# Two heads side by side in a clustered attention kernel: one run of probabilities times v for both

## The chip, the cores and the metric

The kernel runs on one core of one Trainium2 chip. The time is the device time of one execution in microseconds (us); three executions were timed. The core has five engines with queues of their own: TensorE (PE; its weight loads are listed apart as PEld), VectorE (DVE), ScalarE (ACT), GpSimd (POOL) and SyncE (SP), which issues the DMAs here. TensorE writes its results to PSUM, and VectorE and ScalarE carry them from there to SBUF.

## What is computed

```
def _attn_ref(q, k, v, centroids):            # q, k, v: (2, 8, 768, 64)
    ...
    q_assign = np.argmax(np.einsum('bhsd,hcd->bhsc', q_n, c_n), axis=-1)
    k_assign = np.argmax(np.einsum('bhsd,hcd->bhsc', k_n, c_n), axis=-1)
    mask = q_assign[:, :, :, None] == k_assign[:, :, None, :]
    scores = scale * np.matmul(q, k.transpose(0, 1, 3, 2))
    scores = np.where(mask, scores, -1000000000.0)
    ...                                        # softmax over the keys
    return np.matmul(attn, v)
# then x (1536, 512): softmax-gated layer with normalisation (w_in, w_out),
# then (x @ w_a) * (x @ w_b) @ w_out2
```

Every query and key is put to one of 16 clusters of its head; a query sees the keys of its own cluster only. Two feed-forward layers follow.

## The kernel before

Batch 2 and 8 heads make eight pairs of heads `(b, hp)`. A sequence of 768 is six tiles of 128. A step `i` is one query tile `t` of one head `j` of one pair `n`, called a head-tile below; there are 96, and the list `steps` sets their order: before, all six tiles of head 0, then all six of head 1, then the next pair.

A step has these parts. `score`: four matmuls (L992) into one of two PSUM buffers `psS`, with the cluster mask as further rows of the operands; then VectorE takes the negated row maximum (L996) and ScalarE the exponential with its row sum (L1000) into one of two buffers of probabilities. `turn`: six transposes (L1024), three into the PSUM bank `psT0` and three into `psT1` (printed as psT_67 and psT_68, and the score buffers as psS_65 and psS_66); of each step the first half is copied out by VectorE (L1031) and the second by ScalarE (L1033), into a buffer of transposed probabilities at `PT_`. `apply`, for a group of three tiles (384 queries) of one head: part 1 (L1048) multiplies v by the transposed probabilities, six matmuls of 128x384 with 64 output columns, one for each key tile `kt`. They alternate between the two halves of the array's columns, so that even key tiles are summed in PSUM rows 0 to 63 of `psO` and odd ones in rows 64 to 127. Each of these f32 matmuls is two instructions in the profile. Part 2 adds the two half sums: ScalarE copies one (L1061) and VectorE adds the other (L1062). Part 3, once per group of a pair, divides by the row sums (transposes L1077, product L1080) and splits the result into two fp32r parts for the next layer.

Before each pair its queries and keys are prepared (`prep`): loads (L658), transposes (L729 into `psM`; for the very first pair L763), split into a high and a low part (ACT L736, POOL L737 and L739, or DVE L746), similarities to the centroids (L819, L823; for the first pair L788, reduced by L791), the arg-max as one-hot rows (L857 to L874), their transposes (L902, for the first pair L883), and DMAs that place the parts in the operand slots of each head (`do_place`, L805; one-hot rows `do_ohd`, L912). There are four such slots, two pairs of heads.

No order of instructions is written out. Every operation is added to a list with its engine, a cost, a rank, and what it reads and writes (`pl.add`). A list scheduler runs through the list with these costs and takes, on each engine, the operation of lowest rank among those whose inputs are there; what it finds is the program order of each engine. The rank is that of the task (in steps: `SUB`, `LEAD`, `OFF`) plus entries of the table `ADJ`. At run time each engine goes through its list in order and waits at semaphores.

The layers behind attention (`moe_h`, `moe_ln`, `moe_x2`, `moe2_ab`, `moe2_y`; L1139, L1212, L1229, L1282, L1310) keep TensorE busy to the end; weights are split by ScalarE, VectorE and GpSimd before.

## Time and profile before

| | |
|---|---|
| median of three executions | 719.59 us (719.44 to 1163.23) |
| the profiled execution | 717.53 us, span 715.5 us |
| TensorE busy | 697.1 us, 97% of the span |
| VectorE, ScalarE, GpSimd busy | 437.1, 345.4, 264.6 us |
| granted TensorE clock | 0.996 |
| attention ends (last apply run) | about 286 us |

One of the three executions took 1163.23 us; the other two agree within 0.2 us. Busy times are of the profiled execution. A matmul's duration there is the time until its result is there; since matmuls are pipelined, what it costs is read from the distance between the starts of two.

### The profile page before, as it was taken

What the parts mean: (1) busy time and instruction counts of PE and PEld (TensorE: products, weight loads), DVE (VectorE), ACT (ScalarE), POOL (GpSimd) and SP (SyncE); (2) the same over time, 40 slices, a digit from 0 to 9 for tenths busy, and PEclk for the clock granted to TensorE, in tenths of its full rate; (3) what the DMA queues carried; (4) which work ended last, traced back from release to release, by engine and by line L of the source; (5) the groups of instructions that cost most, each with busy time, mean ns of one, the idle gap of its engine ahead of it and who ended that gap; (6) DMA issues with size and microseconds to landing.
All of it is one profiled execution on the core that took longest, in us unless ns stands there. A gap on an engine that the chain in (4) does not pass through costs nothing.

```text
span 715.5 us, 10716 instructions
## 1 busy us (share of the span) xinstructions
PE 697.1 (97%) x3960; PEld 569.0 (80%) x3960; DVE 437.1 (61%) x752; ACT 345.4 (48%) x679; POOL 264.6 (37%) x295
## 2 busy tenths in 40 slices
PE   7898999999999999899999999999999999999997
PEld 6766776787777767788999998888888888888886
DVE  5877777888779868898997269851344211111212
ACT  5766676787777764665356234442242211121111
POOL 2246441456464314557364078950354300000000
PEclk9999999999999999999999999999999999999999
DMA  4647437174716201313223032340020000010011
GB/s 156 155 104 192 133 93 184 49 177 125 204 29 168 70 31 66 112 60 117 89 60 120 1 119 83 124 147 1 22 67 30 1 0 1 0 60 1 20 40 59
DMA packets 39091, 58.46 MB, mean 82 GB/s; under 512 B 3832, under 2 KB 33920, under 8 KB 39040
## 3 DMA queue, kind: packets, MB, share of 16 engines
q1 hardware_dynamic: 39040, 57.79, 28.1%
q8 instruction: 31, 0.51, 0.3%
q14 instruction: 20, 0.16, 0.1%
HBM read 36.74 MB, written 3.15 MB: 56 GB/s over the span
## 4 chain that ended last, share of the span: by engine, by line
PE 83%; DVE 6%; ACT 5%; DMA 2%; issue 1%; SPq 1%; POOL 1%; DVEq 0%; ACTq 0%; POOLq 0%
PE psT L1282 14%; PE psS L1310 14%; PE psS L992 7%; PE psT L1024 7%; PE psO L1282 7%; PE psM L1282 7%; PE psO L1048 7%; PE psS L1139 5%; PE psM L1229 5%; PE psO L1229 5%; ACT F L1000 2%; PE psM L819 1%; PE psT L1212 1%; PE psM L729 1%; DVE mxn L996 1%
## 5 line engine op out<-in xcount | busy, mean ns | idle before, releaser
L472 POOL TENSOR_TENSOR R<-F,R 128x512 fp32r<-128x512 f32 (+1 forms) x68 | 88.0, 1302 | 97.9 <-ACT R L598 77.0
L1282 PE MATMUL psT<-R 128*128 128x512 f32 x432 | 103.5, 389 | 0.0
L1310 PE MATMUL psS<-R 128*128 128x512 f32 x432 | 103.3, 389 | 0.0
L1000 ACT ACTIVATE F<-psS,mxn 128x768 f32<-128x768 f32 x96 | 86.8, 905 | 20.1 <-DVE mxn L996 17.0
L996 DVE TENSOR_REDUCE mxn<-psS 128x1 f32<-128x768 f32 x96 | 90.7, 950 | 7.9 <-PE psS L992 5.3
L1310 PEld LDWEIGHTS psS<-R 128*128 128x128 f32 x432 | 81.1, 188 | 16.8
L1282 PEld LDWEIGHTS psT<-R 128*128 128x128 f32 x432 | 81.0, 188 | 16.7
L992 PE MATMUL psS<-R 128*128 128x512 f32 (+3 forms) x384 | 91.9, 362 | 0.7 <-ACT F L1000 0.7
L1024 PE MATMUL psT<-ident,F 128*128 128x128 f32 x576 | 86.1, 276 | 1.8 <-ACT F L1000 1.4
L589 POOL TENSOR_TENSOR F<-F 128x512 int32<-128x512 int32 x45 | 63.8, 1422 | 34.3 <-DVE F L585 19.6
L1024 PEld LDWEIGHTS psT<-ident,F 128*128 128x128 f32 x576 | 65.4, 141 | 12.8 <-ACT F L1000 7.8
L992 PEld LDWEIGHTS psS<-R 128*128 128x128 f32 (+1 forms) x384 | 65.9, 192 | 11.1 <-ACT F L1000 1.8
L1295 ACT CAST R<-F 128x512 fp32r<-128x512 f32 x36 | 22.5, 624 | 104.1 <-PE psS L1310 102.2
L1296 DVE TENSOR_TENSOR R<-F,R 128x512 fp32r<-128x512 f32 x36 | 32.9, 914 | 64.4 <-ACT R L1295 64.3
L1139 PE MATMUL psS<-R 128*128 128x512 f32 x288 | 68.7, 393 | 2.0 <-DVE F L1160 2.0
L1048 PE MATMUL psO<-F 128*64 128x384 f32 x384 | 69.0, 494 | 0.0
L1139 PEld LDWEIGHTS psS<-R 128*128 128x128 f32 x288 | 53.1, 188 | 13.4 <-DVE F L1160 2.2
L1031 DVE COPY F<-psT 128x384 f32<-128x384 f32 x96 | 52.7, 549 | 12.3 <-PE psT L1024 11.9
L1033 ACT COPY F<-psT 128x384 f32<-128x384 f32 x96 | 45.9, 478 | 27.2 <-PE psT L1024 22.8
L1293 ACT COPY F<-psT 128x512 f32<-128x512 f32 x36 | 21.1, 586 | 66.7 <-PE psT L1282 64.2
L579 POOL TENSOR_SCALAR F<-F 128x512 int32<-128x512 uint32 x45 | 32.5, 722 | 54.5 <-DMA F<-in_moe_w_b_dram 12.3
L1282 PE MATMUL psO<-R 128*128 128x512 f32 x216 | 51.9, 389 | 0.0
(148 smaller groups left out, 1021.4 us busy)
## 6 DMA issues: line engine op xcount, KB each, us to landing
F<-in_moe_w_out_dram SPq DMA_DIRECT2D x20, 512.0 KB, 3.2
R<-R SPq DMA_DIRECT2D x28, 288.0 KB, 4.2
F<-in_moe_w_b_dram SPq DMA_DIRECT2D x12, 512.0 KB, 3.5
F<-in_moe_w_a_dram SPq DMA_DIRECT2D x12, 512.0 KB, 4.0
R<-R SPq DMA_DIRECT2D x28, 192.0 KB, 4.6
F<-in_moe_w_in_dram SPq DMA_DIRECT2D x8, 512.0 KB, 5.1
F<-in_v_dram SPq DMA_DIRECT2D x8, 384.0 KB, 4.5
out_dram<-F SPq DMA_DIRECT2D x12, 256.0 KB, 2.1
```

Source lines behind the costliest of these rows:

```text
L472: pl.add("POOL", pool(n), rank, lambda: G.tensor_tensor(out=out_, in0=in0, in1=in1, op=ALU.subtract), reads, writes)
L589: pl.add("POOL", pool(n), rank, lambda: G.tensor_tensor(out=u, in0=u, in1=low, op=ALU.add), [rk, lwk], [uk])
L992: T.matmul(sp[:, c0:c0 + cn], kq[:r, 2 * m, t * P:(t + 1) * P], kq[:r, 2 * m + 1, c0:c0 + cn], start=m == 0, stop=m == 1)
L996: pl.add("DVE", dve(S), i + SUB["max"], lambda: V.tensor_reduce(out=mxn[:, b:b + 1], in_=sp[:, :S], axis=AX.X, op=ALU.max, negate=True), [ ...
L1000: pl.add("ACT", act(S) + 93 + 93, i + SUB["exp"], lambda: A.activation(F[:, po:po + 768], sp[:, :S], AF.Exp, bias=mxn[:, b:b + 1], scale=1 ...
L1024: T.transpose(sp[:, c, :], pt[:, kt * P:(kt + 1) * P], ident)
L1031: pl.add("DVE", dve(HN), rk, lambda sp=sp, dh=dh: V.tensor_copy(dh, sp), [sk], [hk])
L1048: T.matmul(psO[rs, :AN], vs[:, j, kt % HT * 2 + kt // HT], pt[:, kt, :], start=kt < 2, stop=kt >= NT - 2, tile_position=(0, kt % 2 * D), s ...
L1139: T.matmul(sp[:, n0:n0 + 512], xv5[:, i, a, c], winv[:, w, c, n0:n0 + 512], start=first, stop=(c == KD - 1 and a == 1))
L1229: T.matmul(sp[:, :GN], wo1v(f, w)[:, ds_], d[a][:, f, :], start=(f == 0 and x == 0), stop=(f == NF1 - 1 and x == 2))
L1282: T.matmul(pt, w[:, l, c, :], xv5[:, xs, a, c, :], start=first, stop=(c == KD - 1 and l == 1))
L1310: T.matmul(yv[t][0], hl2[a][:, ts_], wo[:, l, :], start=(first and a == 0 and l == 0), stop=(last and a == 1))
```

## The change

The steps run in another order: three tiles of head 0, the same three of head 1, then the other three of each. The transposed probabilities of the group lie in two buffers, one for each head, where before two buffers were used in turn for consecutive groups. One apply run follows for the group of both heads: twelve matmuls, of which those of head 0 use the first half of the array's columns and those of head 1 the second. Each half of `psO` then holds the whole sum of one head, and part 2 is one ScalarE copy of 128x384. The run's rank puts it directly behind the last turn, where it had been two steps later. Head 1's placing DMAs get an earlier rank. All entries of `ADJ` are other numbers; two stand here for all.

```
-LEAD = {... 'p1': -5.424, ...}
+LEAD = {... 'p1': -8.0, ...}
...
-    "apply1 0 PE": -123.885, "apply1 1 PE": 0.157, "apply1 2 PE": 9.015, "apply1 3 PE": 421.761,
...
-PVC = 6 * 324.0 + 260.0
+PVC = 12 * 324.0 + 260.0
...
-                rk = r0 + LEAD["p1" if j else "p0"] + part * 0.01
+                rk = max(r0 + LEAD["p1" if j else "p0"], 12 * n - 14.0) + part * 0.01
...
-    steps = [(n, j, t) for n in range(NPR) for j in range(2) for t in range(NT)]
+    steps = [(n, j, g * GA + t) for n in range(NPR) for g in range(NG) for j in range(2) for t in range(GA)]
...
-    def pto(n, j, g):
-        return PT_ + (n * 4 + j * 2 + g) % 2 * 2304
+    def pto(j):
+        return PT_ + j * 2304
...
-                for kt in range(NT):
-                    rs = slice(kt % 2 * D, (kt % 2 + 1) * D)
-                    T.matmul(psO[rs, :AN], vs[:, j, kt % HT * 2 + kt // HT], pt[:, kt, :], start=kt < 2, stop=kt >= NT - 2,
-                             tile_position=(0, kt % 2 * D), skip_group_check=True)
-
-            pl.add("PE", PVC, i + SUB["pv"] + 2, mm, [fc((o, NT * AN), (VS[n % 2] + j * 384, 384))], ["psO"], after=70.0)
+                    for j in range(2):
+                        T.matmul(psO[j * D:(j + 1) * D, :AN], vs[:, j, kt % HT * 2 + kt // HT],
+                                 F[:, pto(j) + kt * AN:pto(j) + (kt + 1) * AN], start=kt == 0, stop=kt == NT - 1,
+                                 tile_position=(0, j * D), skip_group_check=True)
+
+            pl.add("PE", PVC, i + SUB["t1"] + 0.1, mm, [fc((PT_, 2 * NT * AN), (VS[n % 2], 768))], ["psO"], after=70.0)
...
-            pl.add("ACT", act(AN) + 110, rk, lambda: A.copy(xv[hi], psO[lo, :AN]), ["psO"], [hk])
-            pl.add("DVE", dve(AN), rk, lambda: V.tensor_tensor(
-                out=xv[hi], in0=psO[hi, :AN], in1=xv[hi], op=ALU.add), ["psO"], [hk])
+            pl.add("ACT", act(AN), i + 3 + SUB["mg"], lambda: A.copy(xv, psO[:, :AN]), ["psO"], [xk])
...
-        if t % GA == GA - 1:
-            task(i + SUB["pv"] + 2, apply, i, 1)
+        if j and t % GA == GA - 1:
+            task(i + SUB["t1"] + 0.1, apply, i, 1)
```

What that does to the order of instructions is shown at three places. The first is TensorE before head 1 of the first pair is scored. Of before, from the similarity transposes of the second pair (L823) to the first apply run; the last score run there (L992) is head 1's first, the seventh of all:

```order
L823 MATMUL psM<-ident,F 128x128 x3
L1024 MATMUL psT_67<-ident,F 128x128 x3
L1024 MATMUL psT_68<-ident,F 128x128 x3
L883 MATMUL psO<-ident,F 64x128 x6
L1024 MATMUL psT_68<-ident,F 128x128 x3
L1024 MATMUL psT_67<-ident,F 128x128 x3
L992 MATMUL psS_65<-R 128x512 x2
L992 MATMUL psS_65<-R 128x256 x2
L1048 MATMUL psO<-F 64x384 x6
```

Of the change, from the same L823 on; the first score run behind L883 is head 1's first, the fourth of all, and the apply run stands 17 rows behind these:

```order
L823 MATMUL psM<-ident,F 128x128 x3
L883 MATMUL psO<-ident,F 64x128 x6
L992 MATMUL psS_66<-R 128x512 x2
L992 MATMUL psS_66<-R 128x256 x2
L992 MATMUL psS_65<-R 128x512 x2
L992 MATMUL psS_65<-R 128x256 x2
L902 MATMUL psM<-ident,F 128x128 x3
L1024 MATMUL psT_67<-ident,F 128x128 x3
```

Three score runs and three turns that stood ahead of L883 now stand behind it.

The second place is VectorE in the same stretch, from the second reduce of head 1's similarities (L791) to the copy of its one-hot rows (L892). Of before:

```order
L791 TENSOR_REDUCE F<-psO 128x2x3x16
L1031 COPY F<-psT_67 128x3x128
L857 TENSOR_REDUCE mx<-F 128x3x4
L859 TENSOR_TENSOR F<-F,mx 128x3x64
L996 TENSOR_REDUCE mxn<-psS_66 128x1
L860 TENSOR_TENSOR F<-F,iot 128x3x64
L746 SCALAR_TENSOR_TENSOR R<-psM,R 128x384
L864 TENSOR_REDUCE mx<-F 128x3x4
L996 TENSOR_REDUCE mxn<-psS_65 128x1
L866 TENSOR_TENSOR F<-F,mx 128x3x4x16
L1031 COPY F<-psT_67 128x3x128
L868 TENSOR_SCALAR F<-F 128x3x2x16
```

Of the change:

```order
L791 TENSOR_REDUCE F<-psO 128x2x3x16
L857 TENSOR_REDUCE mx<-F 128x3x4
L746 SCALAR_TENSOR_TENSOR R<-psM,R 128x384
L859 TENSOR_TENSOR F<-F,mx 128x3x64
L860 TENSOR_TENSOR F<-F,iot 128x3x64
L864 TENSOR_REDUCE mx<-F 128x3x4
L866 TENSOR_TENSOR F<-F,mx 128x3x4x16
L868 TENSOR_SCALAR F<-F 128x3x2x16
L829 TENSOR_REDUCE F<-psM 128x6x32
L892 CAST R<-psO 16x384
```

The row maxima (L996) and the copies of turns (L1031) are gone from between.

The third place is TensorE around an apply run. Of before, the eighth run; the last turn that it needs ended ahead of the piece, three turns earlier:

```order
L992 MATMUL psS_66<-R 128x512 x2
L992 MATMUL psS_66<-R 128x256 x2
L1024 MATMUL psT_68<-ident,F 128x128 x3
L1024 MATMUL psT_67<-ident,F 128x128 x3
L902 MATMUL psM<-ident,F 128x128 x3
L992 MATMUL psS_65<-R 128x512 x2
L992 MATMUL psS_65<-R 128x256 x2
L1024 MATMUL psT_68<-ident,F 128x128 x3
L1024 MATMUL psT_67<-ident,F 128x128 x3
L1077 MATMUL psM<-ident,F 128x128 x3
L1048 MATMUL psO<-F 64x384 x6
```

Of the change, the fourth run; the last turn that it needs is the row psT_68 and the first three transposes of psT_67 directly ahead of it, and the other three are the next step's:

```order
L992 MATMUL psS_65<-R 128x512 x2
L992 MATMUL psS_65<-R 128x256 x2
L1024 MATMUL psT_68<-ident,F 128x128 x3
L1024 MATMUL psT_67<-ident,F 128x128 x6
L1046 MATMUL psO<-F 64x384 x12
L902 MATMUL psM<-ident,F 128x128 x3
L992 MATMUL psS_66<-R 128x512 x2
L992 MATMUL psS_66<-R 128x256 x2
```

The run is twice as long, there are 16 instead of 32, and the work between the last turn and the run has become less.

## Rows read from the trace of the kernel before

**Rows 1.** The page's busy times: us, share of the span, instructions.

```profile
PE 697.1 (97%) x3960; PEld 569.0 (80%) x3960; DVE 437.1 (61%) x752; ACT 345.4 (48%) x679; POOL 264.6 (37%) x295
```

**Rows 2.** Busy us by stretch: PE, PEld, DVE, ACT, POOL, clock, DMA share, GB/s.

```profile
24.00:72.00 48.00, 42.19 (x279) 31.32 (x279) 37.90 (x68) 32.70 (x72) 21.78 (x28) 1.00 0.65 154
72.00:264.00 192.00, 190.11 (x1276) 141.57 (x1272) 155.80 (x262) 142.54 (x311) 85.00 (x103) 1.00 0.44 114
...
288.00:384.00 96.00, 94.05 (x598) 84.74 (x597) 87.81 (x197) 54.02 (x91) 55.27 (x55) 1.00 0.26 88
```

**Rows 3.** VectorE's busy us of lines 996, 1031 and 1062 in the middle stretch.

```profile
72.00:264.00 192.00, 72.69 (x77) 1.00 0.44 114
...
72.00:264.00 192.00, 42.34 (x78) 1.00 0.44 114
...
72.00:264.00 192.00, 14.36 (x26) 1.00 0.44 114
```

**Rows 4.** Groups of instructions, shapes apart: busy us, mean ns | idle before, releasers.

```profile
L996 DVE TENSOR_REDUCE mxn<-psS 128x1 f32<-128x768 f32 x96 | 90.7, 950 | 7.9 <-PE psS L992 5.3 <-ACT F L1000 0.6 <-ACT F L1033 0.3
L1000 ACT ACTIVATE F<-psS,mxn 128x768 f32<-128x768 f32 x96 | 86.8, 905 | 20.1 <-DVE mxn L996 17.0 <-PE psT L1024 1.6 <-PE psS L992 1.1
...
L1048 PE MATMUL psO<-F 128*64 128x384 f32 x384 | 69.0, 494 | 0.0
...
L1031 DVE COPY F<-psT 128x384 f32<-128x384 f32 x96 | 52.7, 549 | 12.3 <-PE psT L1024 11.9
...
L1033 ACT COPY F<-psT 128x384 f32<-128x384 f32 x96 | 45.9, 478 | 27.2 <-PE psT L1024 22.8 <-PE psO L1048 3.3
...
L1000 ACT ACTIVATION_READ_ACCUMULATOR F<-psS,mxn 128x1 f32 x96 | 19.2, 200 | 0.0
L1062 DVE TENSOR_TENSOR F<-psO,F 64x384 f32<-64x384 f32 x32 | 17.7, 553 | 10.0 <-ACT F L1061 9.4
...
L1061 ACT COPY F<-psO 64x384 f32<-64x384 f32 x32 | 15.2, 474 | 6.1 <-PE psO L1048 5.4
```

**Rows 5.** Weight loads in one apply run: start, us, what, idle before.

```profile
102.32 0.14 PEld L1048 LDWEIGHTS psO<-F 128*64 128x64 f32 x2 [0.18 <-issue]
102.64 0.14 PEld L1048 LDWEIGHTS psO<-F 128*64 128x64 f32 x2 [0.18 <-issue]
102.96 0.14 PEld L1048 LDWEIGHTS psO<-F 128*64 128x64 f32 x2 [0.18 <-issue]
```

**Rows 6.** The chain that ended last, around the same run: start, us, what.

```profile
102.01 2.09 PE psO L1048 x12
104.10 0.80 PE psT L1024 x6
...
105.23 0.71 PE psS L992 x4
105.95 0.66 PE psT L1024 x6
```

**Rows 7.** TensorE's instructions in order of time, at the start.

```profile
1.40 2.61 PE L702 MATMUL psO<-ident 128*128 128x128 f32 x11 [1.40 <-POOL ident masks.py:199]
...
30.95 0.49 PE L883 MATMUL psO<-ident,F 128*64 128x128 f32 x3
...
34.23 0.96 PE L992 MATMUL psS<-R 128*128 128x512 f32 x4
```

**Rows 8.** VectorE's instructions in order of time, same stretch.

```profile
23.96 0.56 DVE L791 TENSOR_REDUCE F<-psO 128x96 f32<-128x384 f32 x1
...
25.28 0.69 DVE L859 TENSOR_TENSOR F<-F,mx 128x192 f32<-128x192 f32 x1
25.89 0.95 DVE L996 TENSOR_REDUCE mxn<-psS 128x1 f32<-128x768 f32 x1
...
29.49 0.21 DVE L868 TENSOR_SCALAR F<-F 128x96 f32<-128x96 f32 x1
30.13 0.96 DVE L996 TENSOR_REDUCE mxn<-psS 128x1 f32<-128x768 f32 x1 [0.42 <-ACT F L1000]
```

**Rows 9.** TensorE's waits: us in total, times, longest.

```profile
PE psM L729 <- DMA F<-in_k_dram: 1.6, 1, 1.6
```

**Rows 10.** The chain that ended last, around that load.

```profile
57.93 6.83 DMA F<-in_k_dram
```

More of the change, by code (lines that the diff above doesn't have):

```diff
@@ L19 @@
 ALL = -1
-LEAD = {'t': -15.432, 'sim': -11.595, 'p0': -4.152, 'v': -19.986, 'arg': -8.315, 'p1': -5.424, 'oh': -4.419, 'ohd': -4.097, 'load': -7.494}
+LEAD = {'t': -15.432, 'sim': -11.595, 'p0': -4.152, 'v': -19.986, 'arg': -8.315, 'p1': -8.0, 'oh': -4.419, 'ohd': -4.097, 'load': -7.494}
 GAP = {'t': 0.859, 'sim': 1.308, 'oh': 0.243}
@@ new lines @@
+    "score 6 DVE": -4.268, "score 6 PE": -194.724, "score 7 ACT": 109.288, "score 7 DVE": -34.458,
+    "score 7 PE": 341.777, "score ACT": -27.222, "score DVE": 279.181, "score PE": -0.372,
+    "setup 0 ACT": 64.769, "setup 0 POOL": 38.145, "setup POOL": -71.395, "turn 0 ACT": -36.093,
+    "turn 0 DVE": -32.953, "turn 0 PE": -5.336, "turn 1 ACT": 12.855, "turn 1 PE": 2.178,
+    "turn 2 ACT": 67.026, "turn 2 DVE": 40.368, "turn 2 PE": -0.029, "turn 3 ACT": 52.64,
+    "turn 3 PE": -12.963, "turn 4 ACT": -13.832, "turn 4 DVE": -465.407, "turn 4 PE": -37.715,
```

158 lines of the change are left out of this document (72 added, 86 removed), and 216 rows, old and new, of the table ADJ.

## The prediction, made before the changed kernel was run

> **What bounds the kernel now.** I read the busy times of the whole run first, then the busy times by stretch, then the groups of instructions, then single instructions around one run of probabilities times v. TensorE is busy 97% of the span and no other engine passes 61% [rows 1]. By stretch the picture sharpens [rows 2]: from 72 to 264 us, in the middle of attention, TensorE is idle 192.00 - 190.11 = 1.9 us; from 24 to 72 us it is idle 48.00 - 42.19 = 5.8 us; in the layers behind attention (the third row) VectorE is at 87.81 of 96, yet TensorE misses only 2.0. So what the change is worth is read on TensorE's own time in attention: cycles that it no longer spends, against waits that the new order may add. The steady rate of the middle stretch is 78 head-tiles in 192 us (as many half-copies of VectorE, one per head-tile, stand there [rows 3]), that is 2.46 us per head-tile and 14.8 us per six.
>
> **The apply runs.** The page's 494 ns for one matmul of line 1048 [rows 4] is a latency: two matmuls, one per half of the columns, run at once, and pairs of weight loads stand 0.32 us apart [rows 5]. Six pairs would take 6 x 0.322 = 1.93 us. The run takes 2.09, and the six transposes behind it take 0.80 where six take 0.66 elsewhere [rows 6]. So a run has 2.09 + 0.14 - 1.93 = 0.30 us of entering and leaving. The change keeps all pairs (there are 32 x 6 before, 16 x 12 after, each of one matmul per column half, as now) and halves the number of runs: 16 x 0.30 = **-4.8 us**. The lower bound on this gain would be nothing, if the 0.30 grew with the run's length; the rows speak against that, since the weight loads inside a run are evenly spaced. I take 4.8.
>
> **Moving the result out of PSUM.** Before, a run leaves two half sums: ScalarE copies one (L1061, 474 ns) and VectorE adds the other (L1062, 553 ns), 32 times each [rows 4]. After, one copy of 128 partitions does it, 16 times; the ScalarE copy of 128x384 (L1033) takes 478 ns, so height costs nothing. VectorE loses 32 x 0.553 = 17.7 us, ScalarE 7.6 us. That lies beside a TensorE with 1.9 us of idle time in 192, so little of it reaches the end. Where waits are left, at most 5.8 + 1.9 = 7.7 us can come back [rows 2]. I take **-1.0 us**, bounds 0 and -7.7.
>
> **The start.** Two more warm-up transposes now stand ahead of the first real one; eleven take 2.61 us [rows 7], so two are **+0.5 us** (0.24 each). Then head 1 of the first pair must be ready after three head-tiles instead of six. Before, its first score run starts at 34.23, straight after the two transposes of L883 that began at 30.95 [rows 7]; by then six head-tiles have been scored and turned. In the new order only three have, so three scores and three turns (0.71 and 0.66 us each [rows 6]) are still owed: 4.1 us. Against that, head 1 comes sooner: between the reduce of L791 and the last step L868 of the arg-max, two row maxima of 0.95 us stand in VectorE's way now, and a third one behind L868 at 30.13 [rows 8]; in the new order there is none until head 1's own. The reduce ends at 24.5. Add 0.7 for two more transpose runs of 0.33 that now stand ahead on TensorE, and 2.6 for the seven short operations up to L868 (0.2 to 0.7 each): 27.8. With the 34.23 - 30.95 = 3.3 us from L883 to the score head 1 starts at about 31. That is 3.2 us sooner, so 4.1 - 3.2 = 0.9 remain. The pipe of maximum and exponential has also run dry: the first turn of head 1 waits for score 0.71, maximum 0.95, exponential 0.91 + 0.20 [rows 4] and some 0.2 between, 3.0 us, of which two scores and a transpose run (1.75) cover all but 1.25. Together +2.1. A wait of 1.6 us for a load of k that lands at 64.8 us [rows 9, 10] could swallow part of it, as that load waits on other queues. I take **+1.3 us**, bounds 0 and +4.1.
>
> **The apply's own waits.** It is moved to directly behind the last turn, and it reads both heads' transposed probabilities, which no longer alternate between two buffers. Two things follow. (a) The last copy out of PSUM must be done. The second half of the last tile is read only by the eighth matmul, about 2 us into the run, so only the first half counts: a VectorE copy of 0.55 us plus some 0.15 to start. In 15 of 16 places a score run or as much other work (0.7 us or more) stands between; the fourth has only one transpose run (0.33 us). If the copy queues behind a row maximum it takes 1.65 instead of 0.7, so the bounds are 0 and 16 x 0.6 = 10 us when all do. I take +1.0 by the one thin place and one in five of the others. (b) Copies of the next head-tile must wait for the apply's end, 12 x 0.322 + 0.16 = 4.0 us. In nearly all places a score or a head-preparation run follows the apply, and 0.7 us covers the 0.55 copy: nothing. **+1.0 us** for both.
>
> **Other moves.** Head 1's placing copies are issued earlier on SP's queue. The one-hot DMAs of both heads went out together before in nearly all pairs, so head 1 is on time. The costs written in the planner (PVC, the ranks, ADJ) only set the order. The layers behind attention keep their work. Nothing for these.
>
> **Sum.** -4.8 - 1.0 + 0.5 + 1.3 + 1.0 = -3.0 us. The profiled execution took 717.53 us (a span of 715.5 and 2.0 around it), so 714.5 there; it lies 2.06 below the median of the runs, 719.59. Against that median: 716.6, and I say **716.5 us**.
>
> **Rivals.**
> *Faster by more (evacuation was the limit).* If VectorE's relief returns all of the idle time, -4.8 - 7.7 + 2.8 = -9.7: **709.9 us**. For it: L1061 and L1062 hold VectorE and ScalarE 33 us, and in 24 to 72 us TensorE does wait. Against: VectorE is at 155.80 of 192 in the middle stretch [rows 2], not full. The Trainium skill ("TensorEngine Tiling (Array Packing)", PSUM Bottleneck) says that tiling speeds up TensorE but not the emptying of PSUM, which can become the limit; the trace agrees only for the start, not for the middle stretch. Chance 0.20.
> *Slower (VectorE starved, then swamped).* Between two applies TensorE has 14.8 - 2 x 2.23 = 10.3 us of work per six head-tiles, and issues nothing for the softmax in the 4.0 us of the apply. VectorE needs, per six, 6 x 0.944 for maxima, 6 x 0.543 for copies, and (155.80 - 72.69 - 42.34 - 14.36) / 13 = 2.0 for the rest [rows 2, 3]: 10.9 us. If none of it falls under the apply, TensorE waits 10.9 - 10.3 = 0.6 us per cycle, 16 times: 9.8, and with the start at +4.1, the apply's waits at +1 and the warm-up 0.5: 719.6 - 4.8 + 9.8 + 5.6 = **730 us**; half of it gives 723. It decides as soon as less than 0.6 us of VectorE's work lies under an apply. Before, the applies are 2.1 us, and the softmax of two scored tiles fills them. For the rival: only two score buffers and two probability buffers, so at most two tiles can be ahead, and the buffers of transposed probabilities no longer alternate. Against: two maxima (1.9 us) plus the 2.0 of other work fit under the 4.0. The Trainium skill ("Perfetto Trace Analysis", Optimization Strategy) reads a gap that repeats on the saturated engine as a sign of too few buffers for the next tile; no such repeating gap shows in the trace of before. Chance 0.22.
> *The heads do not overlap on the array.* Then a pair would take 0.64 and the time would rise by 16 x 12 x 0.32 = 61 us, to 780. The same two column halves are used with different moving data in both kernels, so 0.02.
>
> **From these to the numbers.** Forecast (713 to 721) 0.55; faster rival 0.20; slower 0.22; no overlap 0.02; something else 0.01. The range reaches to the faster rival and to the middle of the slower: 709 to 727. A change of this kernel can be told from none at about 2%, 14.4 us: faster than 705.2 needs more than all idle time of attention, 0.03; slower than 734.0 needs the slower rival beyond its worst case, or the third, 0.05; the rest, 0.92, is within.
>
> **What would show it.** Right: 192 logical matmuls of apply in 16 runs of about 3.9 to 4.1 us with the same 0.32 spacing; TensorE idle in 72 to 264 us still near 2 us; head 1's first score near 31 us. The slower rival would show VectorE idle under the applies and score or transpose runs waiting for L1000 or L1031 behind them; a late copy shows as a wait of the apply for L1031. Wrong would be a pair spacing off 0.32, or a first stretch that loses more than 4 us.

## The result, and the profile of the changed kernel

The changed kernel takes **729.12 us** (median of 4 runs, 728.35 to 731.47) where the kernel before, on the same chip, takes 719.52: ratio 1.0145, 95% interval 1.0114 to 1.0177. It is about 10 us slower. The forecast was 716.5, the range 709 to 727: the time lies outside it, on the slow side. The profiled execution has a span of 727.2 us against 715.5, 11.7 us more, which is what the rows below have to account for.

The busy times of the page (us, share of the span, instructions), to be read against [rows 1]:

```profile
PE 703.6 (97%) x3960; PEld 576.4 (79%) x3960; DVE 423.9 (58%) x720; ACT 334.5 (46%) x663; POOL 266.9 (37%) x295
```

VectorE and ScalarE lost the work that the change was to take from them (VectorE 437.1 to 423.9, ScalarE 345.4 to 334.5). TensorE, with the same 3960 matmuls, is busy 6.5 us longer and idle 5 us longer.

By stretch, to be read against [rows 2] (stretch, its length, busy us with instructions of PE, PEld, DVE, ACT, POOL, then the granted clock as a share of 2.4 GHz, DMA share, GB/s):

```profile
24.00:72.00 48.00, 41.46 (x259) 31.21 (x256) 33.23 (x63) 28.42 (x63) 17.71 (x21) 0.93 0.58 142
72.00:264.00 192.00, 185.85 (x1233) 142.49 (x1233) 138.72 (x230) 131.59 (x293) 89.65 (x109) 0.99 0.46 117
```

In the middle stretch TensorE now misses 192.00 - 185.85 = 6.2 us where it missed 1.9, and it gets 1233 instructions done where 1276 were. From 24 to 72 us its granted clock is 0.93, where it was 1.00.

**The runs themselves came out as forecast.** The chain that ended last, around one run of applies (start, us, what), beside [rows 6]:

```profile
81.66 0.38 PE psM L823 x3
82.04 4.02 PE psO L1046 x24
86.06 0.90 PE psM L819 x4
```

Twelve pairs take 4.02 us, that is 12 x 0.322 = 3.86 and 0.16 more. An edge, below, is what entering and leaving a run costs; the rest of it lies ahead of the run and behind it. Worked out from the start times of every matmul around each run, the edges sum to 10.1 us over 32 runs before (0.32 each) and 5.2 us over 16 runs after (0.32 each): **-4.9 us**, for a forecast of -4.8.

**Where the 11.7 us lie.** For every two matmuls that follow each other I took the distance of their starts, less the usual distance of the form (0.227 us for 512 columns, 0.176 for 384, 0.120 for 256, 0.109 for a transpose of 128, 0.161 for an apply). What is over is TensorE's loss; it falls into four kinds:

| us over the usual distance | before | after | difference |
|---|---|---|---|
| at half clock (1.2 GHz) | 1.6 | 8.8 | +7.2 |
| edges of the apply runs | 10.1 | 5.2 | -4.9 |
| idle places over 0.15 us, at full clock | 16.2 | 23.1 | +6.9 |
| the rest (places under 0.15 us) | 8.7 | 11.2 | +2.5 |
| sum | 36.6 | 48.3 | +11.7 |

The idle places at full clock grew by 3.9 us from 48 to 108 us and by 2.7 us from 108 to 264 us; at the start (0 to 48) they are the same within 0.1 us, and behind attention within 0.2. The first row holds everything that is over in a stretch at half clock, waits too. If the clock's part of a matmul there is taken as at most its own usual distance, which doubles, it is 1.5 us before and 5.2 after up to 48 us (+3.7), and the waits up to 48 us, at either clock, grow from 8.5 to 10.8 (+2.3). Of the last row, 2.0 of the 2.5 lie from 108 to 264 us; no run was made for them.

By place, all four kinds together: +4.8 us from 16 to 48 us, -0.4 from 48 to 72, +4.8 from 72 to 108, +1.4 from 108 to 264, where 2.7 and 2.0 us of short waits stand against 3.4 of the edges, and +1.0 behind.

**The start.** The same four stretches, first of the kernel before, then of the changed kernel (columns as above):

```profile
20.00:28.00 8.00, 6.98 (x54) 6.56 (x53) 7.46 (x15) 5.81 (x13) 2.07 (x3) 1.00 0.41 105
28.00:31.00 3.00, 3.00 (x24) 2.74 (x23) 2.51 (x5) 1.74 (x4) 0.00 (x0) 1.00 0.99 252
31.00:35.00 4.00, 2.49 (x18) 1.69 (x15) 3.27 (x8) 3.35 (x7) 0.00 (x0) 1.00 1.11 216
35.00:40.00 5.00, 4.94 (x32) 3.12 (x30) 3.84 (x7) 3.42 (x8) 0.65 (x1) 1.00 0.56 145
```

```profile
20.00:28.00 8.00, 6.41 (x49) 5.59 (x48) 5.98 (x11) 5.63 (x14) 2.63 (x4) 1.00 0.34 96
28.00:31.00 3.00, 1.81 (x10) 1.26 (x10) 2.17 (x7) 0.62 (x3) 0.00 (x0) 1.00 0.98 243
31.00:35.00 4.00, 2.60 (x9) 2.03 (x10) 3.56 (x7) 1.36 (x3) 0.00 (x0) 0.74 1.08 220
35.00:40.00 5.00, 4.40 (x19) 3.59 (x18) 2.58 (x5) 3.69 (x8) 0.66 (x1) 0.53 0.72 186
```

Before, head 0's fourth to sixth query tiles fill TensorE from 28 to 31 us while head 1's q and k are prepared (busy 3.00 of 3.00). After, head 0's first three tiles are done by then and head 1 is what everything waits for: busy 1.81 of 3.00. Behind that the granted clock is 0.74 and then 0.53, that is 1.2 GHz for most of 33 to 40 us. The single instructions of TensorE there (start, us, what, idle before and its releaser):

```profile
28.47 0.94 PE L819 MATMUL psM<-R,cb 128*128 128x384 f32 x4 [0.94 <-DVE R L746]
30.05 0.55 PE L823 MATMUL psM<-ident,F 128*128 128x128 f32 x3 [0.65 <-ACT F L827]
...
32.07 0.52 PE L883 MATMUL psO<-ident,F 128*64 128x128 f32 x3 [1.14 <-DVE R L892]
32.34 0.47 PE L992 MATMUL psS<-R 128*128 128x512 f32 x1
33.14 2.50 PE L992 MATMUL psS<-R 80*128 80x512 f32 x7 [0.33 <-ACT R L894]
36.24 0.90 PE L902 MATMUL psM<-ident,F 128*128 128x128 f32 x3 [0.60 <-DVE F L868]
```

No single idle place there is longer than 1.14 us; there are several within 5 us, and those of 0.33 and 0.60 us fall in the stretch at half clock itself.

**The late loads.** Two pieces of the chain that ended last, in the changed kernel (start, us, what):

```profile
61.39 6.25 DMA F<-in_moe_w_in_dram
67.64 0.02 issue
67.67 0.43 DVE F L572
...
94.48 7.55 DMA F<-in_moe_w_in_dram
102.03 0.02 issue
102.06 0.66 ACT F L567
102.72 0.02 issue
102.74 0.44 DVE F L574
103.18 0.02 issue
103.20 0.69 DVE F L585
103.89 0.48 DVE F L1031
104.37 0.04 issue
104.42 0.80 PE psT L1024 x3
```

These loads are pieces 1 and 2 of w_in, weights of a layer behind attention. They are 512 KB each, and TensorE needs them first at 275.8 us. But VectorE and ScalarE work in their written order, and the preparation of a piece stands in the middle of attention's work: ScalarE waits 4.5 us for piece 2, VectorE 6.3 us for ScalarE, and the copy L1031 that frees a PSUM buffer stands behind. TensorE's longest waits are the result; from the list of waits (us in total, times, longest):

```profile
PE psT L1024 <- DVE F L1031: 5.8, 4, 3.0
```

and the clock pays once more behind the second one, from the changed kernel's stretches:

```profile
64.00:70.00 6.00, 4.34 (x31) 2.94 (x28) 2.33 (x5) 2.71 (x6) 3.39 (x5) 1.00 0.68 215
96.00:104.00 8.00, 5.40 (x33) 2.59 (x31) 1.68 (x4) 2.89 (x8) 1.17 (x3) 1.00 0.77 187
104.00:110.00 6.00, 5.58 (x31) 5.30 (x32) 3.93 (x7) 3.42 (x7) 3.16 (x4) 0.72 0.13 30
```

Why piece 2 is late only now is seen in SP's issues (start, us, what), first before, then after:

```profile
84.74 4.76 SPq L805 DMA_DIRECT2D R<-R  x6
89.60 0.54 SPq L565 DMA_DIRECT2D F<-in_moe_w_in_dram  x1
```

```profile
83.19 5.28 SPq L805 DMA_DIRECT2D R<-R  x6
88.58 0.53 SPq L658 DMA_DIRECT2D F<-in_q_dram  x1
89.29 0.39 SPq L658 DMA_DIRECT2D F<-in_k_dram  x1
89.77 4.67 SPq L805 DMA_DIRECT2D R<-R  x6
94.48 0.60 SPq L565 DMA_DIRECT2D F<-in_moe_w_in_dram  x1
```

The placing copies of both heads and the next q and k now stand together ahead of the piece; it is issued 4.9 us later, and takes 7.55 us to land where it took 5.1.

Piece 1 is another case: it stood behind placing copies, q and k before as well, landed at 67.0 us (67.64 after), and VectorE waited for it then too:

```profile
67.01 0.43 DVE L572 TENSOR_SCALAR F<-F 128x512 f32<-128x512 f32 x1 [2.28 <-DMA F<-in_moe_w_in_dram]
```

TensorE waited 1.6 us for k just before that [rows 9]. So from 48 to 72 us its idle places sum to 2.6 us before and 2.9 after: what is new against the kernel before is nearly all piece 2.

### The profile page after: what moved, and what is told of

The parts are those of the page before. It is cut to its first block, busy times and chain, and to the rows that moved or that the text cites. A ratio compares the mean times of both kernels' runs of the same rounds, so it can differ in the third digit from the quotient of the medians.

```text
span 727.2 us, 10636 instructions
## 1 busy us (share of the span) xinstructions
PE 703.6 (97%) x3960; PEld 576.4 (79%) x3960; DVE 423.9 (58%) x720; ACT 334.5 (46%) x663; POOL 266.9 (37%) x295
## 4 chain that ended last, share of the span: by engine, by line
PE 78%; DVE 8%; DMA 5%; ACT 3%; issue 2%; POOL 2%; SPq 1%; DVEq 0%; POOLq 0%; ACTq 0%
PE psT L1274 13%; PE psS L1302 13%; PE psM L1274 7%; PE psO L1274 7%; PE psO L1046 7%; PE psS L992 7%; PE psT L1024 6%; PE psM L1221 5%; PE psO L1221 5%; PE psS L1131 3%; DMA F<-in_moe_w_in_dram 2%; DMA F<-in_moe_w_out_dram 2%; PE psM L819 1%; DVE mxn L996 1%; PE psM L729 1%
## 5 line engine op out<-in xcount | busy, mean ns | idle before, releaser
L996 DVE TENSOR_REDUCE mxn<-psS 128x1 f32<-128x768 f32 x96 | 91.1, 951 | 26.7 <-PE psS L992 25.6
L992 PE MATMUL psS<-R 128*128 128x512 f32 (+3 forms) x384 | 95.0, 370 | 0.9 <-ACT R L894 0.3
L1000 ACT ACTIVATE F<-psS,mxn 128x768 f32<-128x768 f32 x96 | 86.9, 906 | 15.2 <-DVE mxn L996 11.7
L992 PEld LDWEIGHTS psS<-R 128*128 128x128 f32 (+1 forms) x384 | 67.7, 196 | 14.5 <-ACT F L1000 3.2
L1031 DVE COPY F<-psT 128x384 f32<-128x384 f32 x96 | 52.7, 549 | 24.5 <-PE psT L1024 17.4
L1046 PE MATMUL psO<-F 128*64 128x384 f32 x384 | 65.6, 490 | 0.0
L1286 DVE TENSOR_TENSOR F<-psM,F 128x512 f32<-128x512 f32 x18 | 12.4, 691 | 78.8 <-PE psM L1274 78.8
L1286 DVE TENSOR_TENSOR F<-psO,F 128x512 f32<-128x512 f32 x18 | 12.4, 688 | 72.6 <-PE psO L1274 72.6
L585 DVE SCALAR_TENSOR_TENSOR F<-F 128x512 int32<-128x512 int32 x52 | 52.9, 1024 | 0.4
```

The lines of the kernel that those rows point to most:

```text
L585: pl.add("DVE", dve(n), rank, lambda: V.scalar_tensor_tensor(out=u, in0=topi, scalar=-(2 ** 31), in1=u, op0=ALU.bitwise_and, op1=ALU.bitwi ...
L992: T.matmul(sp[:, c0:c0 + cn], kq[:r, 2 * m, t * P:(t + 1) * P], kq[:r, 2 * m + 1, c0:c0 + cn], start=m == 0, stop=m == 1)
L996: pl.add("DVE", dve(S), i + SUB["max"], lambda: V.tensor_reduce(out=mxn[:, b:b + 1], in_=sp[:, :S], axis=AX.X, op=ALU.max, negate=True), [ ...
L1000: pl.add("ACT", act(S) + 93 + 93, i + SUB["exp"], lambda: A.activation(F[:, po:po + 768], sp[:, :S], AF.Exp, bias=mxn[:, b:b + 1], scale=1 ...
L1046: T.matmul(psO[j * D:(j + 1) * D, :AN], vs[:, j, kt % HT * 2 + kt // HT], F[:, pto(j) + kt * AN:pto(j) + (kt + 1) * AN], start=kt == 0, st ...
```

## The experiments

Theories at the start: **A**, the idle places of the start let the granted clock fall, at about 5 us; **B**, the late pieces of w_in hold up VectorE and ScalarE, at 5 us and 1.5 us of half clock; **C**, the long runs of applies starve VectorE and leave it a heap behind each run. Ratios are to the kernel before, run on the same chip; the changed kernel itself stands at 1.0145. Except where the text says so, the planner makes the changed kernel's order and that order is kept; only what the diff names is moved or put in.

### Start and late weights, first try

The filler is a transpose of the identity into columns of a score buffer that nobody reads, put ahead of TensorE's pieces of work 55 to 62, counted from 0:

```diff
+    FILLERS = {55: 2, 56: 7, 57: 4, 59: 8, 60: 1, 62: 3}
     def emit(self):
-        for i in self.schedule():
-            self.ops[i][3]()
+        idx = self.schedule()
+        n = 0
+        for i in idx:
+            if self.ops[i][0] == "PE":
+                for _ in range(self.FILLERS.get(n, 0)):
+                    self.filler()
+                n += 1
+            self.ops[i][3]()
+    pl.filler = lambda: T.transpose(psS[0][:, 768:896], ident, ident)
```

> The changed kernel with its order of instructions kept on every engine; only 25 more transposes of the identity (0.11 us each at full clock) are put into TensorE's order in the first 36 us, ahead of the places where it stood idle before and at head 1's first score. They fill idle time and compute nothing that is used. Theory A (idle time at the start lets the granted clock fall to half from 32.9 to 39.7 us, which costs some 5 us of work): the clock stays at full speed there, and the time falls by 3 to 5 us, to 724 to 726. Theory B (a weight load that comes late holds up VectorE and ScalarE at 67 and at 97 to 102 us): nothing or at most 1 us, since the late load is not touched. Theory C (the long apply runs starve VectorE and ScalarE everywhere): nothing.

Measured: 728.62 us, ratio 1.0143 [1.0117, 1.0170]. From 16 to 48 us the half clock fell from 5.0 to 0.6 us, as A says. But the 25 fillers cost 2.7 us, and the wait for piece 1 at 67 us ate the rest: from 48 to 72 us TensorE lost 6.0 us instead of 4.1, with half clock behind it. A's mechanism is shown; its price does not show in the time yet.

The second moves the preparation (not the loads) of all eight pieces 6.5 us later in the order, the third adds the fillers:

```diff
+        late = lambda i: self.keys[i] and self.keys[i][-1].rsplit(" ", 1)[0] in ('load_win 0', 'load_win 1', 'load_win 2', 'load_win 3', 'load_win 4', 'load_win 5', 'load_win 6', 'load_win 7') and self.ops[i][0] != "SP"
+        idx.sort(key=lambda i: self.start[i] + (6500 if late(i) else 0.0))
```

> The changed kernel with one difference: what ScalarE, VectorE and GpSimd do to the eight pieces of w_in stands 6.5 us later in their orders; the loads themselves and all other instructions keep their places. Theory B: the waits of VectorE and ScalarE for that load go (4.4 us at 63 to 67.7, 6.3 us at 96.5 to 102.7), with them TensorE's idle 1.8 and 3.2 us behind them, and the half clock at 104.6 to 108: 4 to 7 us less, 722 to 725. Theory A: at most the 1.7 us of the last half-clock stretch. Theory C: nothing.

> Both edits of the two runs above. If A and B each hold a part of the loss, the gains add: 8 to 11 us less, 718 to 721, at or a little below the kernel before, whose runs of apply cost 3.8 us more. Under C the time stays near 729.

Measured: 735.75 us, ratio 1.0236, and 734.92 us, ratio 1.0224. (In both, the last piece is read after a later load has been written over its staging buffer, so part of w_in is other data; the work is the same.) The two places did shrink (48 to 72 us: idle 2.9 to 1.1 us; 72 to 108: the loss 7.8 to 6.1), but a new and larger one came at 249.6 us: the delayed work on the last piece stood behind that later load, in the second VectorE waited 3.0 us for it to land at 250.8, and TensorE lost 4.3 us there, with half clock from 252 to 259 us behind it. Both expectations missed: the delay was put on six pieces that were not late. What the shift costs there says nothing on B.

### How much lies in the fit of the order

The fourth gives the first pair of heads its old arrangement (six tiles of one head, then six of the other, half sums), and lets the planner plan anew with the changed kernel's table of corrections; the eighth keeps the changed kernel and gives the planner the old table.

```diff
-    steps = [(n, j, g * GA + t) for n in range(NPR) for g in range(NG) for j in range(2) for t in range(GA)]
+    OLD = (0,)
+    steps = []
+    for n in range(NPR):
+        if n in OLD:
+            steps += [(n, j, t) for j in range(2) for t in range(NT)]
+        else:
+            steps += [(n, j, g * GA + t) for g in range(NG) for j in range(2) for t in range(GA)]
```

> The changed kernel, but the first pair of heads is worked as in the kernel before (all of head 0, then head 1, four apply runs of one head), pairs two to eight as in the change; the planner then makes its order anew. Theory A: head 1 is not needed early, no half clock after 20 us, 5 to 7 us less. Theory B: what it does to the late loads is open, since the planner's order changes. Theory C: one cycle in eight less, under 1 us.

> The changed kernel with the planner's table of corrections of the kernel before; the planner makes its order anew. Tells how much of the time lies in the table's fit to its list of steps. If the time lies in the new structure (apply runs, pairs of heads) and the table is only fine tuning: within 1% of the changed kernel, 722 to 736 us. If the order is what counts, and a table fitted to another list is worth little: 745 to 790 us, with idle places of TensorE spread over the whole attention part (pair 0 alone in the old arrangement with the changed table gave 777 us).

Measured: 777.07 us, ratio 1.0813 (idle places 66.9 us in all, half clock 14.1), and 757.66 us, ratio 1.0548 (43.2 and 15.3). The changed kernel would take 1.0145 x 718 = 728 us there: with a table that was fitted to another list of steps, 29 us are lost in the eighth, and 48 in the fourth with whatever the first pair's arrangement does. So neither run tells what the first pair's arrangement is worth; they tell that the order has to be kept when one thing in it is tested, which all the others do.

### The two late pieces alone

Fifth: only pieces 1 and 2 are prepared 6.5 us later (their ScalarE, VectorE and GpSimd work, +6500 in the dictionary below). Sixth: their loads are issued 11 us earlier, ahead of the placing copies. Seventh: the sixth with the first experiment's fillers.

```diff
+    MOVE = {'load_win 1 SP': -11000.0, 'load_win 2 SP': -10746.0}
+        def when(i):
+            tag = self.keys[i][-1] if self.keys[i] else ""
+            return self.start[i] + self.MOVE.get(tag, 0.0)
+        idx.sort(key=when)
```

> The changed kernel in its own order, but the work of VectorE, ScalarE and GpSimd on pieces 1 and 2 of w_in is issued 6.5 us later in that order; the loads themselves stay. Nothing else moves. Theory B (the two late loads hold up VectorE and ScalarE, which run in order, and with them the copies of the transposes and the maxima of the scores): TensorE's idle places at 67 us (1.8 us) and 101 us (3.2 us) shrink to under 0.6 us each and the stretch at half clock at 104.6 to 108 us (1.5 us lost) is gone; 6 us less, 723 us (721.5 to 725). Theory C (long runs of applies starve VectorE everywhere): 72 to 264 us hardly change apart from these two places, but neither does the time, since the work only lands between later applies: 727 to 730 us. If only the order's fit counts (every shift in it loses as much as it frees): 728 us or more, with new idle places behind the pieces' new positions.

> The changed kernel in its own order, but the loads of pieces 1 and 2 of w_in are issued ahead of twelve placing DMAs of q and k each on SP's queue (by 11 us of the order) instead of behind them; the work on the pieces stays where it is. Theory B: the pieces have landed when VectorE and ScalarE come to them, the waits of 5.1 us (2) and 4.5 us are gone, TensorE's idle places at 67 and 101 us shrink to under 0.6 us each, and the half clock at 104.6 us goes with them: 723 us (721.5 to 725). Rival: the placing DMAs and the loads of the next heads, now behind 512 KB, are late instead, and the first scores of pairs 2 and 3 wait for them: 727 to 732 us, with waits of TensorE for DMAs at L992 near 74 and 110 us.

> Both: the early loads of pieces 1 and 2, and the 25 filler transposes in TensorE's idle places of the first 36 us (as in the first experiment). Theories A and B together: nothing waits for a load at 67 us any more, so what the fillers won at 16 to 48 us (4.7 us of idle and half clock, against 2.7 us of their own) is no longer swallowed by the wait at 67 us: 720.5 us (718.5 to 723), about 2 us below the early loads alone. If A has no price of its own (the start is bound by the DMAs of pair 1, not by the clock), it equals the early loads alone within 0.6 us.

Measured: 725.90 us, ratio 1.0109 [1.0092, 1.0127]; 722.43 us, 1.0068 [1.0053, 1.0083]; 720.76 us, 1.0040 [1.0026, 1.0054]. The early loads alone take 0.0077 of 718, 5.5 us, off (3 to 8, with the half-widths of the two intervals added as squares). The same three stretches in the sixth, with no idle place and the full clock behind them:

```profile
64.00:70.00 6.00, 6.00 (x47) 5.11 (x44) 5.42 (x9) 5.05 (x12) 5.63 (x7) 1.00 0.35 104
96.00:104.00 8.00, 8.00 (x62) 6.82 (x59) 5.84 (x10) 6.68 (x16) 4.97 (x6) 1.00 0.31 86
104.00:110.00 6.00, 5.97 (x39) 4.32 (x39) 3.92 (x8) 4.30 (x10) 4.12 (x6) 1.00 0.20 46
```

The rival for the sixth (placing copies late instead) did not come: the first score run of no pair waits for a DMA. B is shown, with its price; that it is more than the waits that the change added has to do with piece 1, whose wait the kernel before had in another form. The fifth got only 2.6 us, less than B's expectation and more than C's: at those two places TensorE is busy throughout, but in that profile its half clock is longer at the start (10.5 us in all, against 8.8), and some of the idle time stands elsewhere. In the seventh the fillers are worth another 0.0028 x 718 = 2.0 us, as expected (0.5 to 3.5 in the same way): 5.5 us less at half clock with its waits (1.9 in all against 7.4 in the sixth), and the fillers' own 2.7 us more. These two traces alone do not carry the price, since 3.1 of the 3.6 us between them lie behind the last apply run, where nothing was changed. Over more traces it holds: in the five without fillers whose order is the same up to there (the changed kernel, the fifth, sixth, tenth and fifteenth) the first apply run starts at 43.9 to 45.2 us, in the first and the seventh at 42.8 and 43.1, some 1.7 us sooner. The start of the seventh, to be held against the rows above:

```profile
28.00:31.00 3.00, 2.79 (x22) 2.47 (x22) 2.00 (x6) 0.94 (x2) 0.00 (x0) 1.00 0.99 251
31.00:35.00 4.00, 2.83 (x17) 1.96 (x15) 3.73 (x7) 0.94 (x2) 0.00 (x0) 1.00 1.10 212
35.00:40.00 5.00, 3.99 (x27) 3.34 (x27) 3.45 (x7) 4.09 (x10) 0.65 (x1) 1.00 0.63 168
```

With TensorE busy 2.79 of 3.00 from 28 to 31 us the clock stays at 2.4 GHz to 40 us: A is shown too, with its price. The Trainium skill ("TensorE: Matmul & The Clock Gate", HAM oscillation — how this bites in real kernels) describes bursts of matmuls with waits for DMA between them that lower the clock, and lets the loss be paid anew at each. The traces here agree that it is paid anew, at 33 us and at 104 us; at 104 us the chain goes back to a late load, while at 33 us the waits are for VectorE and ScalarE and none is longer than 1.14 us.

The control, early loads in the kernel before (its own order, pieces 1 and 2 moved by 11 and 9 us):

> The kernel before, in its own order, with the loads of pieces 1 and 2 of w_in issued ahead of placing DMAs (by 11 and 9 us of the order), as the changed kernel had them in the sixth experiment. Tells whether the gain of the early loads (5.9 us there) belongs to the changed order or to any order. If the late pieces are a matter of the changed order alone: within 0.3% of the kernel before (VectorE's wait of 2.3 us for piece 1 at 67 us goes, but TensorE's idle places at 63.0 and 67.9 us wait for the k load, which now lies behind piece 1 and may come later): 716 to 720. If both kernels lose to these loads alike: 712 to 714 us.

Measured: 720.85 us, ratio 1.0031 [1.0013, 1.0048]: nothing gained, 2 us lost. TensorE's waits for loads grew there (2.3 us for k instead of 1.6, and 1.7 for q); the chain shows the load of k (start, us, what):

```profile
60.14 8.15 DMA F<-in_k_dram
```

against 6.83 in [rows 10]. So the gain of the early loads belongs to the changed order.

### What an edge costs

The prediction's largest term rests on the price of leaving and entering a run. The tenth puts one transpose into the middle of each run (an edge more, 16 times), the eleventh the same transpose ahead of each run, among other transposes (none more):

```diff
                 for kt in range(NT):
+                    if kt == NT // 2:
+                        T.transpose(psO[:, AN:AN + P], ident, ident)
                     for j in range(2):
```

> The changed kernel with one transpose of 128x128 (into columns of psO that nobody reads) in the middle of each of the 16 runs of 24 applies, so that each run is left and entered once more: the price of an edge, on which the prediction's largest term (-4.8 us for 16 edges) rests. If an edge costs the time that the trace shows (0.30 us and the transpose's 0.11): 16 x 0.41 = 6.6 us more than the changed kernel's 728 to 729, 735 us (733.5 to 736.5). If an edge is covered by what TensorE waits for anyway (it lies in front of a wait for VectorE or ScalarE): under 3 us more.

> The same 16 transposes, each directly ahead of its run, behind other transposes: no further edge. Beside the split runs it takes away what the transposes themselves cost: 16 x 0.11 = 1.8 us more than the changed kernel, 730 us (729 to 731.5); the difference to the split runs is then 16 edges, 4.8 us by the trace's 0.30.

Measured: 731.53 us, ratio 1.0198 [1.0161, 1.0235], and 729.91 us, ratio 1.0158 [1.0136, 1.0180]. (The transpose in the middle falls into psO's bank while the run's sums are open there: the Trainium skill, "PSUM — Partial Sum Buffer", PSUM: the matmul accumulator, says that a second sum opened in a bank where one is still open makes the next matmul of the first overwrite instead of add. By that rule the tenth's outputs lack half of each sum; the times do not show it.) In the tenth's trace a split run stands as

```profile
145.19 2.16 PE L1048 MATMUL psO<-F 128*64 128x384 f32 x12
147.28 0.33 PE L1046 MATMUL psO<-ident 128*128 128x128 f32 x1
147.53 2.16 PE L1048 MATMUL psO<-F 128*64 128x384 f32 x12
149.62 0.55 PE L729 MATMUL psM<-ident,F 128*128 128x128 f32 x3
```

From 145.19 to 149.62 are 4.43 us, against 4.02 of the unsplit run: 0.41, a transpose and 0.30, as expected. But 16 x 0.30 is 4.8 us, and the two kernels differ by 1.6 by their medians and 2.9 by their ratios, whose intervals overlap. The tenth has no stretch at half clock behind 104 us, which costs the eleventh 1.5, and its idle places outside the edges sum to 2.3 us less. I read that as an edge ahead of a wait for a late load taking from that wait; the times alone do not settle the price.

The fifteenth asks the same without late loads, and tests C: on the sixth's order each run is cut in two halves, and the piece of work behind the run goes between them.

```diff
-                for kt in range(NT):
+                for kt in range(half * HT, half * HT + HT):
...
+            if pe and self.keys[i] and self.keys[i][0] == "apply1 PE":
+                self.ops[i][3](0)
+                rest = i
+                continue
             self.ops[i][3]()
+            if pe and rest is not None:
+                self.ops[rest][3](1)
+                rest = None
```

> The changed kernel with the early loads of pieces 1 and 2 (722.4 us beside 717.9 of before, ratio 1.0068), and each run of 24 applies cut into two of 12, with the one piece of TensorE work that follows the run (3 to 4 transposes or matmuls, 0.3 to 0.8 us) moved between the halves. It puts back the 16 edges (0.30 each in the trace: 4.8 us) and gives VectorE and ScalarE their next work 2 us earlier. If the long runs starve VectorE and ScalarE and leave them a heap behind each run, TensorE's short idle places at 108 to 264 us (5.0 us in the sixth experiment's trace, 2.2 in the kernel before) fall to 3 us or less, and the time rises by 2 to 3 us only: ratio 1.010. If these idle places come from the order's fit and not from the runs' length, they stay near 5 us and the time rises by the full 4 to 5 us: ratio 1.013.

Measured: 728.63 us, ratio 1.0137 [1.0114, 1.0160]. Against the sixth's 1.0068 that is 0.0069 of 718, 5.0 us (3 to 7 in the same way): the full price of 16 edges (in its trace 11.3 us of them in 32 runs, 5.2 in the sixth's 16; the profiled execution has 2.7 us more of half clock besides, and 2.3 us less of other idle places). The idle places from 108 to 264 us did not fall: 5.6 us, against 5.0 in the sixth, so the second of its expectations came. The sign that the prediction named for C, VectorE idle under the applies, is there in the changed kernel, and the fifteenth did not take it away (72 to 264 us; line, busy us, mean ns | idle before, releasers; first before, then after, then the fifteenth, where the row maximum is L1012):

```profile
L996 DVE TENSOR_REDUCE mxn<-psS 128x1 f32<-128x768 f32 x77 | 72.7, 950 | 6.4 <-PE psS L992 4.4 <-ACT F L1033 0.3 <-PE psT L1024 0.3
```

```profile
L996 DVE TENSOR_REDUCE mxn<-psS 128x1 f32<-128x768 f32 x75 | 71.1, 950 | 18.6 <-PE psS L992 17.7 <-ACT F L1000 0.2
```

```profile
L1012 DVE TENSOR_REDUCE mxn<-psS 128x1 f32<-128x768 f32 x74 | 70.1, 950 | 25.5 <-PE psS L1008 24.2 <-PE psT L1040 0.5
```

The piece that went between the halves is a score run in only one of the 16 places, and preparation, transposes or the next layer's work in the others, so VectorE's next row maximum hardly came sooner. Idle time of VectorE alone is no loss, but the fifteenth leaves C untested where it matters: what it shows is the price of an edge. What makes the 2.7 us of short idle places from 108 to 264 us, and the 2.0 us in places under 0.15 us there, is left open, and C stays one candidate for them; with all loads moved forward (below) 4.2 to 4.4 us remain of the 5.0 in idle places.

### What is left

Ninth: all pieces 1 to 7 loaded 7 to 11 us earlier, 12 fillers. Thirteenth: the same, 25 fillers and 25 more at 8, 11 and 13 us, where TensorE waits for the centroids. Sixteenth and seventeenth: 25 early fillers, and 25 or 12 late ones that wait for nobody. Fourteenth: the control, 36 fillers in the kernel before. The thirteenth's lists:

```diff
+    FILLERS = {55: 2, 56: 7, 57: 4, 59: 8, 60: 1, 62: 3, 31: 10, 34: 10, 35: 5}
+    MOVE = {'load_win 1 SP': -11000.0, 'load_win 2 SP': -10746.0, 'load_win 3 SP': -7000.0, 'load_win 4 SP': -8000.0, 'load_win 5 SP': -8000.0, 'load_win 6 SP': -8000.0, 'load_win 7 SP': -8000.0}
```

> The changed kernel in its own order with the loads of all pieces 1 to 7 of w_in issued 7 to 11 us earlier on SP's queue, and 12 filler transposes instead of 25 at the same idle places of the first 36 us. If 12 fillers still keep TensorE's granted clock up at 32 to 39 us, they cost 1.3 instead of 2.7 us; and the wait of VectorE for piece 5 (1.1 us at 174 us, with 0.9 us of TensorE behind it) goes: 2 us below the 25 fillers with pieces 1 and 2, 718.5 us (717 to 720), level with the kernel before. If 12 are too few, the half clock returns at 32 to 39 us and it stands at 721 to 722.5, as the early loads without fillers.

> The changed kernel with the loads of pieces 1 to 7 of w_in issued early and 50 filler transposes: the 25 of the first experiment and 25 more in TensorE's idle places at 8, 11 and 13 us, where it waits for the centroids and the first loads. If what is left of the loss is half clock (5.1 us of it with 12 fillers, at 11.4 to 18.2 and 35.3 to 38.7 us, against 1.6 in the kernel before), it falls under 2 us here, and the time to 717.5 (716 to 719), level with the kernel before or 0.5 us under it. If the fillers themselves take what the clock gives back (25 late ones cost 2.7 us), it stays at 719.5 to 721.

> As the thirteenth experiment (all loads of w_in early, 50 fillers), but the 25 late fillers write to the other score buffer, as in the first experiment, so that none of them waits for ScalarE's reading of a score: in the thirteenth's trace they stood behind the waits at 27 and 33 us, not in them. If that misplacement cost 1 to 2 us: ratio 0.997 to 0.999. If fillers cost their own time wherever they stand: as there, 1.000.

> As the one before, with 12 late fillers instead of 25. If the clock holds at 32 to 39 us thanks to the 25 early fillers, 1.3 us less than with 50: ratio 0.996 to 0.998, a shade faster than the kernel before. If it falls again at 35 us (2.7 us lost in the ninth experiment): ratio 1.000 to 1.002.

> The kernel before in its own order with 36 filler transposes in TensorE's idle places at 8, 11, 26.7 and 31.4 us, which are the same waits (centroids, first loads, head 1's q and k). Its granted clock is at half at 13.7 to 17.1 us only (1.4 us lost) and stays up behind 26.7 and 31.4 us, since work of head 0's later query tiles stands ahead of the waits. If fillers gain only where the clock falls: 1 us gained at most, 717 to 718.5 where the kernel before has 718; if fillers behind 26 us only stand in the way: 718.5 to 720.

| run | us | ratio, 95% interval | half clock, us | fillers, us |
|---|---|---|---|---|
| ninth | 719.69 | 1.0024 [1.0009, 1.0039] | 5.1 | 12 x 0.109 = 1.3 |
| thirteenth | 719.63 | 0.9998 [0.9984, 1.0013] | 0.0 | 5.5 |
| sixteenth | 718.50 | 1.0004 [0.9994, 1.0013] | 0.0 | 5.5 |
| seventeenth | 718.39 | 1.0002 [0.9992, 1.0013] | 1.5 | 4.0 |
| fourteenth (of before) | 723.16 | 1.0056 [1.0043, 1.0069] | 0.0 | 3.9 |

With 12 late fillers and no early ones the clock falls at 11 us and again at 35 us, and the ninth's ratio stays above the others; its time is in the range of its first expectation, though the clock fell as in its second. With the loads early and the clock held, the changed kernel is level with the kernel before; none of these runs is faster. Fillers buy back the clock and little more: the thirteenth's misplaced ones (they stood behind ScalarE's reading of a score) cost nothing beside the sixteenth's, by the ratios, as its second expectation has it. In the kernel before, whose clock hardly falls, 36 of them made it 4.0 us slower, more than either expectation; in its trace the last apply run starts 2.6 us later (286.4 against 283.8), and the rest lies behind attention, where nothing was changed. So in the changed kernel the fillers put back about what the 16 edges gave; a version that beats both would need real work in those idle places, and was not found.

## Why the prediction was wrong, by its own steps

- **The apply runs, -4.8.** Right: 4.9 us by the edges in the trace, and 5.0 us (3 to 7) in time when the fifteenth puts them back. The bound "nothing, if the 0.30 grew with the run's length" is out.
- **Moving the result out of PSUM, -1.0.** The work went (VectorE 13.2 us, ScalarE 10.9 us less busy; forecast 17.7 and 7.6), the time did not: TensorE's idle time in the middle stretch rose from 1.9 to 6.2 us. Relief of engines with room to spare gave nothing that shows; the upper bound of 7.7 was no bound of this change, since the waits in it are of other kinds, the longest for the load of k [rows 9].
- **The start, +0.5 and +1.3.** The wait was sized about right: head 1's first score stands at 32.34 (forecast near 31), the first one of all 0.48 us later, and the waits up to 48 us, at either clock, grew by 2.3 us (forecast 1.3, beside 0.5 for the warm-up). The step that failed is that it **counted only waiting time**. Sparser work ahead of the wait took the clock to 1.2 GHz, and the doubled distances added 3.7 us. From 16 to 48 us the kernel lost 4.8 us more than before, over the bound of +4.1, in rows that [rows 2] could only show at 1.00.
- **The apply's own waits, +1.0.** Too much by most of it: 12 of 16 runs have edges of 0.304 to 0.310 us, and all 16 together 0.3 us more than that price, so no late copy.
- **"Other moves ... Nothing for these."** This is the second failed step. The placing copies of both heads and q and k now stand ahead of piece 2's 512 KB load on SP's queue; ScalarE, working in order, waits 4.5 us for it, and TensorE behind it 3.2 us, with 1.5 us of half clock: 4.8 us in all from 72 to 108 us. For piece 1 VectorE waits 4.4 us and TensorE loses 1.8, as much as it lost to the load of k there before. With both loads moved forward, 5.5 us came back. The prediction followed the moved DMAs to their own readers (head 1 is on time) and not to what is queued behind them.
- **The slower rival** named 730 us, nearly the time that came, but by another mechanism (VectorE starved under the applies). Its sign is in the rows; a price for it was not shown, and halved runs, which left VectorE as idle, do not rule it out. That 4.7 us of short waits, 2.7 in idle places and 2.0 under 0.15 us each, appeared with the new order from 108 to 264 us is measured; their cause is open, and they are half of the 9.8 us that this rival put there. That the time came near 730 is luck.
- **The faster rival** (evacuation as the limit) falls with the second point; **no overlap of the heads** falls with the run of 4.02 us for twelve pairs.
- **The range** ended at 727, the middle of the slower rival. The causes that were not thought of sum to 7.2 us at half clock (waits there included) and 3.9 us of idle places from 48 to 108 us.

## What to carry to other kernels

A gain worked out on the bound engine (here 4.9 us of edges) holds only as long as the rest of an order that was fitted around the old structure still fits: for each moved step ask what is queued behind it, on the DMA queue and on each engine that works in order, even when the thing moved is early enough for its own reader. At a place where the bound engine waits, ask also how much work stands ahead of the wait; if the change thins it out, add the price of the lower clock behind it (here 3.7 us, beside waits that grew by 2.3). And hold the order still when testing: a planner run anew with a table fitted to another list moved the time by 29 to 48 us, more than anything under test.

## What the runs showed of the hardware

- TensorE's granted clock fell to 1.2 GHz behind several idle places of at most 1.14 us each with little work between them (busy 1.81 of 3.00 us), and stayed at 2.4 GHz where 25 transposes stood in them (busy 2.79 of 3.00).
- Filler transposes in idle places are not free: 36 of them, 0.11 us each, made the kernel before 4.0 us slower, 2.6 of it by the last apply run in its trace. In the changed kernel 25 of them, 2.7 us of their own, made it 2.0 us faster, by what the clock gave back.
- A 512 KB load issued behind placing copies and loads of q and k took 6.25 and 7.55 us from issue to landing (6.9 and 5.1 in the kernel before), with the DMA share at 0.95 in the second:

```profile
94.00:102.00 8.00, 6.75 (x43) 3.66 (x41) 2.44 (x5) 2.49 (x5) 2.54 (x4) 1.00 0.95 203
```
